# Two feed-forward steps moved ahead of the last attention products, and tiles placed on 64-byte multiples

## The chip, the cores and the metric

The kernel runs on one core of a Trainium2 chip. The metric is the time of one execution on the device in microseconds (us), as the median of several runs. The engines are named as in the profile: PE is TensorE (matmuls; PEld are its weight loads), DVE is VectorE, ACT is ScalarE, POOL is GpSimd, and SP is SyncE, whose queue issues every transfer here.

## The reference

Attention with pooled queries feeds a two-layer feed-forward part. Cut to what matters:

```python
# q, k, v: (8, 8, 1152, 64) float32
q_pool = q.reshape(B, H, S // 2, 2, D).mean(axis=3)          # 576 queries
scores = (q_pool @ k.transpose(0, 1, 3, 2)) / np.sqrt(D)
scores = scores - np.max(scores, axis=-1, keepdims=True)
attn = np.exp(scores)
attn = attn / (np.sum(attn, axis=-1, keepdims=True) + 1e-09)
x = (attn @ v).transpose(0, 2, 1, 3).reshape(4608, 512)      # tokens x d_model
h = x @ w_in                                                 # w_in: 512 x 2048
g = h - np.tanh(h)
out = g @ w_out                                              # w_out: 2048 x 512, out: 4608 x 512
```

## The kernel before

**Attention (lines 155 to 484).** Two heads of one batch make a pair, so there are 32 pairs, worked one after the other. A pair has 18 places: two halves of 288 queries times nine tiles of 128 keys. In the first 18 places each place makes a score tile (`scores`: four matmuls a head, in tiles `kq_h`, `kq_l`, `m_row`, `sel`), ACT takes the exponential into a tile p, and POOL adds the p tiles by threes into six tiles `sum` (`add_p`, twelve additions in all). In the second 18 places come the products with v: for each half, nine key tiles times two heads go into one PSUM tile o, which ACT copies out (`pv_out`, tile `o_s`) and SP stores to `x_dram`. After them the sums of p over the keys are made with 24 matmuls (`sums`), which need POOL's six tiles; ACT copies them out (`s_s`) and SP stores them.

All these PSUM tiles come from one ring of four tiles of 128 x 2 x 512 float32 (`psum`, line 183); a fifth tile takes the place of the first and waits until the last reader of the first is done. Between the places, other work runs from a table (`add`, `run`): the maxima of the next pairs' scores, loads, and the splitting of the weights into a high and a low part by DVE and ACT (class `W`, tiles `w_raw`, `w_off`, `w_t`, `w_hl`). In the pairs 28 to 31 the table also brings in what the feed-forward part needs first: x of chunk 0 (class `X`), which is read back from `x_dram`, divided by the sums and split into `x_h` and `x_l` (done in pair 30), and the weights of the first five steps, which are loaded into tiles whose work is over (`first_weights`): step 0 into `w_raw`, step 1 into `w_off`, step 2 into `w_hl`, steps 3 and 4 into `w_t`, `raw` and `q2`.

**Feed-forward (lines 487 to 611).** The 4608 tokens are worked in nine chunks of 512, each with 16 steps, one for every 128 columns of `w_in`: 144 steps in all. A step has a first product, 12 matmuls of 512 columns into `ps_h` (`hidden`: x_h and x_l are the moving operands, the weights the stationary ones); then h - tanh(h) (`shrink`), on ACT the square `g_u`, two more squares `g_s` and the tanh `g_t`, on POOL a mask `g_m`, on DVE six instructions, of which the fifth (a subtraction, `g_t` from `ps_h`) is the last that reads h and the sixth (a predicated copy) needs the mask; then the result is split into `g_hi` (ACT) and `g_lo` (POOL), one step later; and two steps later the second product, 12 matmuls into four tiles `ps_o` (`second`: g_hi and g_lo are stationary, the weights `wo` move). `ps_h` and a scratch `ps_w` have two tiles each, `ps_o` four. PSUM is given to them only when the ring is closed. At the start of this part SP loads the other 22 weight tiles (`wt`, tile `w`). x of chunk c + 1 is fetched in step 4 of chunk c and prepared on POOL and ACT in steps 7 to 14. x of even chunks lies in pool `xp0`, opened ahead of attention, and x of odd chunks in `xp1`, opened behind it. The last step works in two halves of 256 tokens.

**Order.** Every engine's instructions are held in the order in which the program issues them (`InOrder`, line 27). All instructions are issued through that wrapper, so the profile puts them all on line 37; they are told apart by their tiles.

**Places in SBUF.** Pools are laid out in the order in which they are opened, each tile padded to a multiple of 32 bytes per partition. The order at the bottom is `pc` (two float32), `xp0`, two tiles `x_r`, two tiles `rec` (36 float32 each), `w_raw`, `w_off` (4100 two-byte words), `w_t`, `w_hl`, `raw`, `q2`, and then attention's own pools, whose place the feed-forward part's pools take over later.

Of the kernel before, what the change touches and what calls it, by code (L numbers as in the profile page):

```python
# [7 lines left out]
F32 = mybir.dt.float32  # L8
F32R = mybir.dt.float32r
I32 = mybir.dt.int32  # L10
U16 = mybir.dt.uint16
AF = mybir.ActivationFunctionType
# [34 lines left out]
def attention_ffn_kernel(  # L47
# [30 lines left out]

    const = ctx.enter_context(tc.tile_pool(name="const", bufs=1))
    dram = ctx.enter_context(tc.tile_pool(name="scratch", bufs=1, space=DRAM))  # L80
    pc = const.tile([P, 2], F32, name="pc")
    nc.vector.memset(pc[:, 0:1], A1)
    nc.vector.memset(pc[:, 1:2], A2)

# [25 lines left out]
    class X:  # L110


        def __init__(self, ci):
            self.t0, self.n = chunks[ci]
            self.h = xp[ci % 2].tile([P, NP, 512], F32R, name="x_h")
            self.l = xp[ci % 2].tile([P, NP, 512], F32R, name="x_l")
            self.r = {}
# [24 lines left out]
    rc = {}  # L142

    def fetch_sums(b):
        rc[b] = rcp.tile([P, NP * 2 * SQ // P], F32, name="rec")
        sp.dma_start(rc[b], s_dram[b].rearrange("a h (x n) -> (a h x) n", n=NP * 2 * SQ // P))

    def reciprocals(b):

        dve.tensor_scalar(rc[b], rc[b], 1e-9, None, op0=ALU.add)  # L150
        dve.reciprocal(rc[b], rc[b])
        sp.dma_start(r_dram[b].rearrange("a h (x n) -> (a h x) n", n=NP * 2 * SQ // P), rc[b])


    with ExitStack() as actx:
# [27 lines left out]
        def psum():  # L183
            return ring.tile([P, 2, 512], F32, name="ps")
# [134 lines left out]
        class W:  # L319
# [3 lines left out]
            def load(self):  # L323
                self.raw = wp.tile([P, WN, 2], I32, name="w_raw")

                self.off = wp.tile([P, 4 * WN + 4], U16, name="w_off")
                for dst in (self.raw.rearrange("p n w -> p (n w)").bitcast(U16), self.off[:, 1:4 * WN + 1]):
                    if self.kind == 0:
                        rs, cs = slice(self.i * P, (self.i + 1) * P), slice(4 * self.c, 4 * (self.c + WN))
                        sp.dma_start(dst, w_in[rs, cs])  # L330
                    else:
                        rs = slice(self.i * P, (self.i + 2) * P)
                        sp.dma_start(dst.rearrange("p (a n) -> p a n", a=2), w_out[rs].rearrange("(a p) n -> p a n", a=2))
                self.hw = self.raw[:, :, 1]
                self.mid = self.off[:, 0:4 * WN].bitcast(I32).rearrange("p (n w) -> p n w", w=2)[:, :, 1]
# [123 lines left out]
        def run(pi, place):  # L459
            while at.get((pi, place)):  # L460
                at[pi, place].pop(0)()

        for pi in range(n_pair):
            w = pairs[pi]
            ps = [Half(), Half()]
            for place in range(NS):
                half, kt = divmod(place, KT)
                ps[half].append(scores(w, half, kt))
                add_p(ps[half], half, kt)
                run(pi, place)  # L470
            for place in range(NS):
                half, kt = divmod(place, KT)
                if kt == 0:
                    o = psum()
                for h in range(2):
                    tiled(o[:, 0, 0:HQ], w.v[:, kt, h], ps[half][kt][:, h], h, start=(kt == 0), stop=(kt == KT - 1))
                if kt == KT - 1:
                    pv_out(w, half, o)
                run(pi, NS + place)
                if pi >= 2 and place in (3, 6, 11, 15) and work:  # L480
                    work.pop(0)()
            sums(w, ps)
            run(pi, 2 * NS)
# [1 line left out]


    wt = ctx.enter_context(tc.tile_pool(name="wt", bufs=1))
    gp = ctx.enter_context(tc.tile_pool(name="gp", bufs=2))
    ps_h = ctx.enter_context(tc.tile_pool(name="ps_h", bufs=2, space=PSUM))
    ps_w = ctx.enter_context(tc.tile_pool(name="ps_w", bufs=2, space=PSUM))  # L490
    ps_o = ctx.enter_context(tc.tile_pool(name="ps_o", bufs=4, space=PSUM))
    LAG = 2

    for f in range(NF):
        for which, have in enumerate((wi, wo)):
            if f not in have:
                load_w(wt.tile([P, 1024], F32R, name=f"w{which}_{f}"), f, which)
    xp.append(ctx.enter_context(tc.tile_pool(name="xp1", bufs=1)))

    class Step:  # L500
        pass

    def hidden(s):

        s.h = ps_h.tile([P, 512], F32, name="ps_h")
        mm = [(w, x, c) for w, x in ((0, s.x.h), (0, s.x.l), (1, s.x.h)) for c in range(NP)]
        for k in s.parts:
            for j, (w, x, c) in enumerate(mm):
                pe.matmul(s.h[:, k], wi[s.f][:, w, c], x[:, c, k], start=(j == 0), stop=(j == len(mm) - 1))

    def g_high(s, k=slice(0, 512)):
        act.activation(s.g_h[:, k], s.s1[:, k], AF.Copy)

    def g_low(s, k=slice(0, 512)):
        pool.tensor_tensor(s.g_l[:, k], s.s1[:, k], s.g_h[:, k].bitcast(F32), op=ALU.subtract)

    def shrink(s, before):
        t = lambda name, dt=F32: gp.tile([P, 512], dt, name=name)
        all_ = t("g_u"), t("g_t"), t("g_s1"), t("g_s2"), t("g_m", mybir.dt.uint8), ps_w.tile([P, 512], F32, name="ps_w")
        s.s1 = all_[2]  # L520
        s.g_h = gp.tile([P, 512], F32R, name="g_hi", bufs=LAG + 1)
        s.g_l = gp.tile([P, 512], F32R, name="g_lo", bufs=LAG + 1)
        for k in s.parts:
            shrink_part(s, before, s.h[:, k], *(a[:, k] for a in all_))
            before = None

    def shrink_part(s, before, h, u, th, s1, s2, m, w):
        act.activation(u, h, AF.Square)
        act.activation(s1, u, AF.Square, bias=pc[:, 0:1])
        act.activation(s2, u, AF.Square, bias=pc[:, 1:2])  # L530
        act.activation(th, h, AF.Tanh)
        if before:
            g_high(before)
        pool.tensor_scalar(m, u, T_POLY * T_POLY, None, op0=ALU.is_ge)
        if before:
            g_low(before)
        dve.scalar_tensor_tensor(w, u, -P0, h, op0=ALU.add, op1=ALU.mult)
        dve.scalar_tensor_tensor(w, u, PL, w, op0=ALU.mult, op1=ALU.mult)
        dve.scalar_tensor_tensor(w, s1, P1, w, op0=ALU.add, op1=ALU.mult)
        dve.scalar_tensor_tensor(s1, s2, P2, w, op0=ALU.add, op1=ALU.mult)  # L540
        dve.tensor_tensor(th, h, th, op=ALU.subtract)
        dve.copy_predicated(s1, m, th)

    def second(s, js):
        po = s.chunk.po
        for j in js:
            if len(po) <= j:
                po.append(ps_o.tile([P, DM], F32, name="ps_o"))
            ts = slice(j * P, (j + 1) * P)
            for i, (g, w) in enumerate(((s.g_h, 0), (s.g_h, 1), (s.g_l, 0))):  # L550
                pe.matmul(po[j], g[:, ts], wo[s.f][:, w], start=(s.f == 0 and i == 0), stop=(s.f == NF - 1 and i == 2))

    def store(c, j):
        o = gp.tile([P, DM], F32, name="o_f", bufs=4)
        act.activation(o, c.po[j], AF.Copy)
        sp.dma_start(out[c.t0 + j * P:c.t0 + (j + 1) * P], o)

    class Chunk:
        pass

    def halves():
        return [slice(0, 256), slice(256, 512)]

    steps = []
    xs = x0[0]
    nxt = None
    for ci in range(len(chunks)):
        c = Chunk()
        c.t0, c.po = chunks[ci][0], []
        for f in range(NF):  # L570
            s = Step()
            s.x, s.f, s.chunk, s.parts = xs, f, c, [slice(0, 512)]
            steps.append(s)
        if ci == len(chunks) - 1:
            s.parts = halves()
        xs = None
        for f in range(NF):
            n = ci * NF + f
            s = steps[n]
            hidden(s)  # L580
            if ci + 1 < len(chunks):
                if f == 4:
                    nxt = X(ci + 1)
                    nxt.fetch()
                if f in (4, 5, 9, 11):
                    nxt.fetch_r((4, 5, 9, 11).index(f))
            if n >= 2:
                second(steps[n - 2], range(4))
            shrink(s, steps[n - 1] if n else None)
            if f == 1 and ci:  # L590
                for j in range(4):
                    store(steps[n - 2].chunk, j)
            if n == 4:
                fetch_sums(B - 1)
            if n == 6:
                reciprocals(B - 1)
            if ci + 1 < len(chunks) and 7 <= f < 7 + 2 * NP:
                if f % 2:
                    nxt.times(pool, (f - 7) // 2)
                    nxt.high((f - 7) // 2)  # L600
                else:
                    nxt.low(pool, (f - 7) // 2)
        xs = nxt
# [46 lines left out]
```

## Time and profile before

| | |
|---|---|
| median of 3 runs | 1632.63 us (1632.5 to 1632.68) |
| the profiled execution | 1633.7 us; span 1631.9 us from the first to the last instruction |
| mean granted TensorE clock | 0.996 |
| PE busy | 1586.2 us, 97% of the span |
| DVE, POOL, ACT busy | 1280.5, 1113.3 and 938.5 us |
| attention ends, feed-forward begins | at about 824.9 us |
| transfers | 166.15 MB, mean 102 GB/s |

A row of a timeline gives the start and the length in us, the engine, the line, the operation, the tiles as out<-in, and in brackets the idle time of the engine ahead of it with what ended it. A row of a chain gives start, length and the piece of work. Buffer numbers are left out of names, so `w` stands for each of the 22 tiles loaded late, and `g_s` for `g_s1` and `g_s2`. Matmuls overlap in the profile: the time of a group is read from its start to the start of the next.

### The profile page before, as it was taken

Reading aid. Unit: us, or ns where it says so; the run is one execution under the profiler, and the core shown is the slowest. Engines: PE = TensorE matmul, PEld = TensorE weight load, DVE = VectorE, ACT = ScalarE, POOL = GpSimd, SP = SyncE. Lnnn points to the kernel's source line nnn. Section 1 sums busy time; section 2 is a strip of 40 time slices with the busy share of each in tenths; the row PEclk is TensorE's granted clock in tenths of the full one; section 3 lists DMA queues with packets and bytes.
Section 4 is the critical chain, followed back from the end, with each engine's and each line's share of the span. In section 5 each row is a group of like instructions: output and inputs, shape, how many; then the busy total and the mean of one; then the engine's idle time right before and its main releaser. Section 6 shows DMA issues by size and latency. Waiting matters only on the chain.

```text
span 1631.9 us, 30673 instructions
## 1 busy us (share of the span) xinstructions
PE 1586.2 (97%) x12012; PEld 1228.4 (75%) x12012; DVE 1280.5 (78%) x1621; ACT 938.5 (58%) x1584; POOL 1113.3 (68%) x749
## 2 busy tenths in 40 slices
PE   5999999999999999999999999999999999999998
PEld 4777676776776776777768888888888888888886
DVE  6788888898889898969447777777777777777776
ACT  3565565565655656656535656555555656555554
POOL 3777786776767767778756666666757675666654
PEclk9999999999999999999999999999999999999999
DMA  4335444344453554333471101001010101020000
GB/s 169 107 119 197 167 150 182 133 183 162 155 214 135 200 182 160 131 123 100 152 310 34 65 7 48 31 7 65 13 65 14 65 14 65 13 65 10 30 1 26
DMA packets 79602, 166.15 MB, mean 102 GB/s; under 512 B 11874, under 2 KB 38498, under 8 KB 77410
## 3 DMA queue, kind: packets, MB, share of 16 engines
q1 hardware_dynamic: 79458, 164.20, 28.3%
q8 instruction: 94, 1.54, 0.4%
q14 instruction: 50, 0.41, 0.1%
HBM read 126.12 MB, written 38.04 MB: 101 GB/s over the span
## 4 chain that ended last, share of the span: by engine, by line
PE 83%; DVE 11%; DMA 2%; issue 2%; ACT 2%; POOL 0%; SPq 0%; POOLq 0%; DVEq 0%; ACTq 0%
PE ps L37 35%; PE ps_h L37 24%; PE ps_o L37 24%; DVE mx L37 3%; DVE w_t L37 3%; DVE kq_l L37 1%; DVE w_hl L37 1%; DMA wi_dram<-w_hl 1%; DVE raw L37 1%; ACT w_t L37 1%; DMA m_dram<-tr 0%; SPq L37 0%; DMA q<-in_q_dram 0%; ACT q_last L37 0%; POOL sum L37 0%
## 5 line engine op out<-in xcount | busy, mean ns | idle before, releaser
L37 DVE TENSOR_REDUCE mx<-ps 128x2 f32<-128x768 f32 x448 | 396.6, 924 | 86.9 <-PE ps L37 85.0
L37 POOL TENSOR_TENSOR sum<-p,p 128x576 f32<-128x576 f32 x192 | 300.6, 1566 | 196.7 <-ACT p L37 196.5
L37 ACT ACTIVATE p<-ps 128x576 f32<-128x576 f32 x576 | 353.2, 653 | 112.1 <-PE ps L37 93.7
L37 POOL TENSOR_SCALAR g_m<-g_u 128x512 uint8<-128x512 f32 (+1 forms) x145 | 250.6, 1728 | 197.6 <-ACT g_u L37 182.5
L37 POOL TENSOR_TENSOR sum<-sum,p 128x576 f32<-128x576 f32 x192 | 301.1, 1568 | 29.2 <-ACT p L37 15.1
L37 PE MATMUL ps<-kq_h 64*128 64x288 f32 (+1 forms) x1920 | 289.3, 345 | 28.0 <-DVE mx L37 17.6
L37 PE MATMUL ps<-p,v 128*64 128x288 f32 x2304 | 286.4, 407 | 0.1
L37 DVE SCALAR_TENSOR_TENSOR ps_w<-g_u,ps_h 128x512 f32<-128x512 f32 (+1 forms) x145 | 100.4, 693 | 191.3 <-ACT g_t L37 191.2
L37 PEld LDWEIGHTS ps<-p,v 128*64 128x64 f32 x2304 | 162.6, 137 | 114.4 <-ACT p L37 6.9
L37 POOL TENSOR_TENSOR g_lo<-g_s,g_hi 128x512 fp32r<-128x512 f32 (+1 forms) x145 | 186.6, 1287 | 89.5 <-ACT g_hi L37 89.5
L37 PE MATMUL ps_o<-w,g_hi 128*128 128x512 f32 x792 | 244.5, 390 | 1.0 <-ACT g_hi L37 1.0
L37 PEld LDWEIGHTS ps<-kq_h 64*128 64x128 f32 x1920 | 181.3, 187 | 80.8 <-DVE mx L37 33.0
L37 ACT ACTIVATE g_u<-ps_h 128x512 f32<-128x512 f32 (+1 forms) x145 | 85.8, 591 | 244.0 <-PE ps_h L37 242.3
L37 PE MATMUL ps_h<-x_h,w 128*128 128x512 f32 (+1 forms) x800 | 214.8, 390 | 0.0
L37 ACT ACTIVATE g_s<-g_u,pc 128x512 f32<-128x512 f32 x290 | 193.2, 714 | 11.3
L37 PEld LDWEIGHTS ps_h<-x_h,w 128*128 128x128 f32 x800 | 149.6, 188 | 32.4
L37 PEld LDWEIGHTS ps_o<-w,g_hi 128*128 128x128 f32 x792 | 148.5, 188 | 33.6 <-ACT g_hi L37 1.4
L37 PE MATMUL ps<-kq_l,kq_h 64*128 64x288 f32 x1152 | 171.8, 295 | 0.0
L37 PE MATMUL ps<-kq_h,kq_l 64*128 64x288 f32 x1152 | 171.5, 294 | 0.0
L37 PE MATMUL ps<-m_row,sel 64*128 64x288 f32 x1152 | 171.2, 293 | 0.0
L37 PE MATMUL ps_o<-w,g_lo 128*128 128x512 f32 x396 | 154.8, 391 | 0.6 <-POOL g_lo L37 0.5
L37 DVE COPY_PREDICATED g_s<-g_m,g_t 128x512 f32<-128x512 uint8 (+1 forms) x145 | 108.4, 748 | 15.0
(92 smaller groups left out, 2368.3 us busy)
## 6 DMA issues: line engine op xcount, KB each, us to landing
raw<-in_k_dram SPq DMA_DIRECT2D x32, 576.0 KB
q<-in_q_dram SPq DMA_DIRECT2D x32, 576.0 KB
v<-in_v_dram SPq DMA_DIRECT2D x32, 576.0 KB
x_dram<-o_s SPq DMA_DIRECT2D x32, 288.0 KB
x_l<-x_dram SPq DMA_DIRECT2D x9, 1024.0 KB
out_dram<-o_f SPq DMA_DIRECT2D x36, 256.0 KB
w_raw<-in_w_in_dram SPq DMA_DIRECT2D x8, 1024.0 KB
w_off<-in_w_in_dram SPq DMA_DIRECT2D x8, 1024.0 KB
```

What stands on the lines that cost most here:

```text
L37: i = f(*args, **kwargs)
```

## The change

Two things are changed. First, three tiles get larger sizes, so that every tile starts at a multiple of 64 bytes: `pc` from 8 to 64 bytes, `rec` from 144 to 192 (of which the same part is used), `w_off` from 8200 to 8256.

Second, in the last pair the first product and `shrink` of steps 0 and 1 are issued between the scores and the products with v. Their h and their scratch come from the ring, one ring tile with two halves for the two h, and one for the two scratch tiles, so the last stage takes five ring tiles in place of three. The functions of the feed-forward part and the pool `gp` of its SBUF tiles move ahead of attention, and the feed-forward loop leaves out the two steps' first product and `shrink`. Their second products stay where they were, in steps 2 and 3.

```diff
-    pc = const.tile([P, 2], F32, name="pc")
+    pc = const.tile([P, 16], F32, name="pc")
...
-        rc[b] = rcp.tile([P, NP * 2 * SQ // P], F32, name="rec")
+        rc[b] = rcp.tile([P, 48], F32, name="rec")[:, 0:NP * 2 * SQ // P]
...
+    gp = ctx.enter_context(tc.tile_pool(name="gp", bufs=2))
...
+    class Step:
+        def __init__(self, x, f, chunk):
+            self.x, self.f, self.chunk, self.parts = x, f, chunk, [slice(0, 512)]
...
-                self.off = wp.tile([P, 4 * WN + 4], U16, name="w_off")
+                self.off = wp.tile([P, 4 * WN + 32], U16, name="w_off")
...
+        steps = []
         for pi in range(n_pair):
...
                 run(pi, place)
+            if pi == n_pair - 1:
+                c = Chunk(0)
+                steps = [Step(x0[0], f, c) for f in range(NF)]
+                h, u = psum(), psum()
+                for n in range(2):
+                    steps[n].h, steps[n].w = h[:, n], u[:, n]
+                    hidden(steps[n])
+                    shrink(steps[n], steps[n - 1] if n else None)
             for place in range(NS):
...
     wt = ctx.enter_context(tc.tile_pool(name="wt", bufs=1))
-    gp = ctx.enter_context(tc.tile_pool(name="gp", bufs=2))
...
     for ci in range(len(chunks)):
-        c = Chunk()
-        c.t0, c.po = chunks[ci][0], []
-        for f in range(NF):
-            s = Step()
-            s.x, s.f, s.chunk, s.parts = xs, f, c, [slice(0, 512)]
-            steps.append(s)
+        if ci:
+            c = Chunk(ci)
+            steps += [Step(xs, f, c) for f in range(NF)]
...
-            hidden(s)
+            if n >= 2:
+                s.h, s.w = ps_h.tile([P, 512], F32, name="ps_h"), ps_w.tile([P, 512], F32, name="ps_w")
+                hidden(s)
...
             if n >= 2:
                 second(steps[n - 2], range(4))
-            shrink(s, steps[n - 1] if n else None)
+                shrink(s, steps[n - 1])
```

More of the change, by code (lines that the diff above doesn't have):

```diff
@@ L152, in reciprocals, with hidden @@
         sp.dma_start(r_dram[b].rearrange("a h (x n) -> (a h x) n", n=NP * 2 * SQ // P), rc[b])
+    gp = ctx.enter_context(tc.tile_pool(name="gp", bufs=2))
+    LAG = 2
+    class Step:
+        def __init__(self, x, f, chunk):
+            self.x, self.f, self.chunk, self.parts = x, f, chunk, [slice(0, 512)]
+    def hidden(s):
+        mm = [(w, x, c) for w, x in ((0, s.x.h), (0, s.x.l), (1, s.x.h)) for c in range(NP)]
+        for k in s.parts:
+            for j, (w, x, c) in enumerate(mm):
+                pe.matmul(s.h[:, k], wi[s.f][:, w, c], x[:, c, k], start=(j == 0), stop=(j == len(mm) - 1))
@@ new lines, in g_high, with g_low, shrink @@
+    def g_high(s, k=slice(0, 512)):
+        act.activation(s.g_h[:, k], s.s1[:, k], AF.Copy)
+    def g_low(s, k=slice(0, 512)):
+        pool.tensor_tensor(s.g_l[:, k], s.s1[:, k], s.g_h[:, k].bitcast(F32), op=ALU.subtract)
+    def shrink(s, before):
+        t = lambda name, dt=F32: gp.tile([P, 512], dt, name=name)
+        all_ = t("g_u"), t("g_t"), t("g_s1"), t("g_s2"), t("g_m", mybir.dt.uint8), s.w
+        s.s1 = all_[2]
+        s.g_h = gp.tile([P, 512], F32R, name="g_hi", bufs=LAG + 1)
+        s.g_l = gp.tile([P, 512], F32R, name="g_lo", bufs=LAG + 1)
+        for k in s.parts:
+            shrink_part(s, before, s.h[:, k], *(a[:, k] for a in all_))
+            before = None
@@ new lines, in shrink_part @@
+    def shrink_part(s, before, h, u, th, s1, s2, m, w):
+        act.activation(u, h, AF.Square)
+        act.activation(s1, u, AF.Square, bias=pc[:, 0:1])
+        act.activation(s2, u, AF.Square, bias=pc[:, 1:2])
+        act.activation(th, h, AF.Tanh)
+        if before:
+            g_high(before)
+        pool.tensor_scalar(m, u, T_POLY * T_POLY, None, op0=ALU.is_ge)
+        if before:
+            g_low(before)
+        dve.scalar_tensor_tensor(w, u, -P0, h, op0=ALU.add, op1=ALU.mult)
+        dve.scalar_tensor_tensor(w, u, PL, w, op0=ALU.mult, op1=ALU.mult)
+        dve.scalar_tensor_tensor(w, s1, P1, w, op0=ALU.add, op1=ALU.mult)
+        dve.scalar_tensor_tensor(s1, s2, P2, w, op0=ALU.add, op1=ALU.mult)
+        dve.tensor_tensor(th, h, th, op=ALU.subtract)
+        dve.copy_predicated(s1, m, th)
@@ new lines, in second, with store @@
+    def second(s, js):
+        po = s.chunk.po
+        for j in js:
+            if len(po) <= j:
+                po.append(ps_o.tile([P, DM], F32, name="ps_o"))
+            ts = slice(j * P, (j + 1) * P)
+            for i, (g, w) in enumerate(((s.g_h, 0), (s.g_h, 1), (s.g_l, 0))):
+                pe.matmul(po[j], g[:, ts], wo[s.f][:, w], start=(s.f == 0 and i == 0), stop=(s.f == NF - 1 and i == 2))
+    def store(c, j):
+        o = gp.tile([P, DM], F32, name="o_f", bufs=4)
+        act.activation(o, c.po[j], AF.Copy)
+        sp.dma_start(out[c.t0 + j * P:c.t0 + (j + 1) * P], o)
@@ L155, in attention_ffn_kernel, with __init__, halves @@
+    class Chunk:
+        def __init__(self, ci):
+            self.t0, self.po = chunks[ci][0], []
+    def halves():
+        return [slice(0, 256), slice(256, 512)]
     with ExitStack() as actx:
@@ L491, in attention_ffn_kernel @@
     ps_o = ctx.enter_context(tc.tile_pool(name="ps_o", bufs=4, space=PSUM))
-    LAG = 2
     for f in range(NF):
@@ L498, in attention_ffn_kernel @@
     xp.append(ctx.enter_context(tc.tile_pool(name="xp1", bufs=1)))
[L500 to L566, printed above, removed]
-    for ci in range(len(chunks)):
-        c = Chunk()
-        c.t0, c.po = chunks[ci][0], []
-        for f in range(NF):
-            s = Step()
-            s.x, s.f, s.chunk, s.parts = xs, f, c, [slice(0, 512)]
-            steps.append(s)
+    xs = nxt = None
+    for ci in range(len(chunks)):
+        if ci:
+            c = Chunk(ci)
+            steps += [Step(xs, f, c) for f in range(NF)]
@@ L574, in attention_ffn_kernel @@
         if ci == len(chunks) - 1:
-            s.parts = halves()
+            steps[-1].parts = halves()
         xs = None
```

## Prediction

> **What bounds the kernel now.** I read the page first, for the engine that sets the end.
>
> ```profile
> span 1631.9 us, 30673 instructions
> ...
> PE 1586.2 (97%) x12012; PEld 1228.4 (75%) x12012; DVE 1280.5 (78%) x1621; ACT 938.5 (58%) x1584; POOL 1113.3 (68%) x749
> ...
> PE 83%; DVE 11%; DMA 2%; issue 2%; ACT 2%; POOL 0%; SPq 0%; POOLq 0%; DVEq 0%; ACTq 0%
> ```
>
> TensorE is busy 97% of the span and is 83% of the chain that ended last. So two things can save time: shorter matmuls, and less idle TensorE. The second view is that chain in order of time, around the border of chunk 0 and chunk 1 of the feed-forward part (start, length, what). A piece of 12 matmuls named ps_h is one step's first product, ps_o the second product of the step two before.
>
> ```profile
> 909.35 2.81 PE ps_h L37 x12
> ...
> 914.89 2.79 PE ps_h L37 x12
> ...
> 925.93 2.72 PE ps_h L37 x12
> 928.65 2.80 PE ps_o L37 x12
> ...
> 942.46 2.72 PE ps_h L37 x12
> ```
>
> The reader is to see that equal work takes two lengths. The piece at 909.35 is the last step of chunk 0 and takes 2.81, and 942.46 in chunk 1 takes 2.72. In between, the first step of chunk 1 (weights in w_raw) takes 2.79, the third (weights in w_hl) 2.72; then the second product of step 0 of the chunk, whose moving operand is w_raw, takes 2.80. The groups of TensorE's instructions between 848.2 and 1608 us, shapes apart, say the same (last: busy us, mean ns):
>
> ```profile
> L37 PE MATMUL ps_o<-w_hl,g_hi 128*128 128x512 f32 x72 | 22.2, 390 | 0.0
> ...
> L37 PE MATMUL ps_o<-w_raw,g_hi 128*128 128x512 f32 x64 | 20.1, 396 | 0.0
> L37 PE MATMUL ps_o<-w_off,g_hi 128*128 128x512 f32 x64 | 20.1, 396 | 0.0
> ```
>
> Three sets of tiles are slow: x of the even chunks, w_raw and w_off. By the code's sizes (each padded to 32 bytes, as in the program's list of tiles) pc takes 32 bytes and starts at 16512, so x of the even chunks starts at 16544, w_raw at 37344, w_off at 45536: all 32 past a multiple of 64. w_off is 8224 bytes long, which ends that: w_t, w_hl and everything behind, x of the odd chunks too, lie on multiples of 64. A moving operand is 512 x 4 = 2048 bytes per partition: 32 blocks of 64 bytes, or 33 when it starts half a block off. 33/32 is 1.031, and 2.81/2.72 is 1.033. Blocks of 128 or 256 bytes would give 17/16 = 1.06 or 9/8 = 1.13. So I read the excess as one more 64-byte block per matmul.
>
> The other loss is the handover from attention to the feed-forward part, again from the chain, with the granted clock of one stretch (third number from the end) under it:
>
> ```profile
> 824.94 3.08 PE ps_h L37 x12
> ...
> 833.58 0.61 DVE g_t L37
> 834.19 0.04 issue
> 834.24 5.49 PE ps_h L37 x12
> 839.72 3.06 PE ps_o L37 x12
> 842.79 2.81 PE ps_h L37 x12
> ```
> ```profile
> 833.00:840.50 7.50, 6.26 (x15) 0.54 1.03 419
> ```
>
> Step 2's first product starts at 834.24, when VectorE has last read step 0's result, and then takes 5.49 instead of 2.81, because the clock stood at half (0.54). The chain loses a wait of 3.4 us and 3 us of slow matmuls.
>
> **The change, part 1: multiples of 64.** pc becomes 64 bytes, rec 192, w_off 8256; x, w_raw and w_off then start on multiples of 64. From step 3 of chunk 0 the chain is TensorE's alone up to the last step:
>
> ```profile
> 1608.71 2.81 PE ps_h L37 x12
> ```
> ```profile
> 1614.25 2.87 PE ps_h L37 x24
> ```
>
> From 842.79 (step 3) to 1608.71 (step 142) are 765.92 us for 139 steps. At 2.72 + 2.72 = 5.44, which the odd chunks already show beside the same work on the other engines, they take 756.16: **9.76 us less**. The last step's two halves (2.87) can give 0.15 more, of which I take 0.1, since ScalarE and VectorE set the time from there on. Attention's matmuls lie on multiples of 64 already: nothing. The weights' preparation reads w_raw and w_off on ScalarE and VectorE, each by single 4-byte words 8 bytes apart; no row has such a read at another place. I take 0; for the bounds see the range.
>
> **Part 2: two steps ahead of the last products with v.** Rows of the handover, by engine:
>
> ```profile
> 813.86 8.95 PE L37 MATMUL ps<-p,v 128*64 128x288 f32 x72
> 822.75 1.66 PE L37 MATMUL ps<-sum,ones 128*32 128x288 f32 x24
> 824.94 1.20 PE L37 MATMUL ps_h<-x_h,w_raw 128*128 128x512 f32 x4 [0.53 <-ACT s_s L37]
> ...
> 827.84 0.40 PE L37 MATMUL ps_h<-x_h,w_off 128*128 128x512 f32 x1
> ...
> 842.63 1.09 PE L37 MATMUL ps_h<-x_h,w_t 128*128 128x512 f32 x4
> ```
> ```profile
> 822.13 1.41 POOL L37 TENSOR_TENSOR sum<-sum,p 128x576 f32<-128x576 f32 x1
> ...
> 828.85 1.49 POOL L37 TENSOR_SCALAR g_m<-g_u 128x512 uint8<-128x512 f32 x1 [5.31 <-ACT g_u L37]
> ```
> ```profile
> 834.28 0.74 DVE L37 COPY_PREDICATED g_s<-g_m,g_t 128x512 f32<-128x512 uint8 x1
> ...
> 837.71 0.68 DVE L37 TENSOR_TENSOR g_t<-ps_h,g_t 128x512 f32<-128x512 f32 x1
> ```
>
> Now: from 813.86 to step 3's first matmul at 842.63, 28.77 us. After, on TensorE in order: two first products 2 x 2.72 = 5.44; the products with v 822.75 - 813.86 = 8.89; a new wait W; the sums up to the next start, 824.94 - 822.75 = 2.19 (the wait for s_s stays); step 2's first product 2.72 + 0.09 (the start behind a gap: 827.84 - 824.94 = 2.90 against 2.81); second product 2.72. Together 22.05 + W.
>
> W is the price. The ring has four tiles; the stage now takes five (h, u, two o, sums), so the sums get h's place and need step 1's last read of h, VectorE's subtraction. That stands behind step 0's copy_predicated, which needs g_m, which GpSimd computes only behind its twelve sums: 822.13 + 1.41 = 823.54, plus g_m 1.49 = 825.03. From the copy to the end of the next subtraction are 837.71 + 0.68 - 834.28 = 4.11, with two hand-overs of 0.04 ("issue" above) 829.2. TensorE gets there at 813.86 + 5.44 + 8.89 = 828.19. **W = 1.0**; between 0 (GpSimd ready earlier) and 1.5, as g_m also takes 1.95:
>
> ```profile
> 868.62 1.95 POOL L37 TENSOR_SCALAR g_m<-g_u 128x512 uint8<-128x512 f32 x1 [1.90 <-ACT g_u L37]
> ```
>
> The handover takes 23.05: **5.7 us less**. On ScalarE, g_hi of step 0 waits for the same copy (about 825.9) with both copies out of o and s_s behind it; the first of these is needed by nobody before the feed-forward part's tiles, the others are not ready earlier anyway. VectorE is idle all through the products with v now. On SyncE the order stays, but s_s, and the 22 weight loads behind it, move with the sums, 829.2 - 822.75 = 6.5 us back:
>
> ```profile
> 825.53 0.39 SPq L37 DMA_DIRECT2D w<-wi_dram  x1
> ...
> 845.70 0.32 SPq L37 DMA_DIRECT2D w<-wo_dram  x1
> 846.94 0.37 SPq L37 DMA_DIRECT2D x_l<-x_dram  x1
> ```
> ```profile
> 872.23 1.29 POOL L37 TENSOR_TENSOR x_r<-x_l,x_r 128x512 f32<-128x512 f32 x1
> ```
>
> The 22 loads come 0.96 us apart (20.17/21) where a step of 5.44 uses two, and the first is used only by step 5, so they stay ahead. x of chunk 1 is then fetched at 853.4, and GpSimd takes it up about 6 us earlier than 872.23, near 866. That leaves 12 us for 1024 KB, 2.5 us at the 419 GB/s of the clock's row above. Covered. Moving gp outside the attention stage costs no instruction.
>
> **Sum.** 9.76 + 0.1 + 5.7 = 15.6 us. The profiled execution took 1633.7 (span 1631.9); less 15.6 is 1618.1. The median of the runs, 1632.63, lies 1.07 below that execution: **1617.0**.
>
> **The rivals.**
> D: the clock halves in the new handover, at W and the wait for s_s. Idle stretches of TensorE of 1.5 us did this in attention (a wait of the stretch from 400 to 410 us, and the clock of that stretch and of one more):
>
> ```profile
> PE ps L37 <- DVE mx L37: 1.5, 1, 1.5
> ```
> ```profile
> 400.00:410.00 10.00, 8.43 (x91) 0.83 0.57 209
> 478.00:488.00 10.00, 8.44 (x86) 0.83 0.74 278
> ```
>
> 0.17 of 10 us is 1.7 us lost each time. One or two such: 1618.7 to 1620.4. [...]
>
> A: step 1's first product waits for step 0's readers of h, as both lie in one tile. For it: the last step's first half on ScalarE began only when both halves were written.
>
> ```profile
> 1617.14 0.39 ACT L37 ACTIVATE g_u<-ps_h 128x256 f32<-128x256 f32 x1 [2.56 <-PE ps_h L37]
> ```
>
> Against it: those halves share 2048 bytes, h's two are 2048 apart. Price: TensorE idles from its product's end to the end of VectorE's subtraction, 834.19 - (824.94 + 3.08) = 6.2, and again runs slow for 5.49 - 2.81 + 3.06 - 2.80 = 2.9, while W vanishes: 31.1 instead of 28.77, so 9.9 - 2.3 = 7.6 gained: 1625.0.
>
> B: the place is not what makes these tiles slow, so part 1 does nothing. For it: the slow tiles are also the lowest in memory, which the trace can't part from their offset. Against: the ratio of 33/32. Then only the handover gains, 28.77 - (2 x 2.81 + 8.89 + 2.19 + 2.90 + 2.80 + 0.9) = 5.5: 1627.1. [...]
>
> C, on the other side: what counts is a multiple of 256. All fast tiles of the feed-forward part lie on such now (w_t at 53760 = 210 x 256). The change moves everything from w_t on by 32 + 64 + 32 = 128 bytes (gp alters nothing: 2 x (4 x 2048 + 512) + 6 x 2048 + 4 x 2048 = 37888 = 148 x 256): every step is slow, 2.81 + 2.81 = 5.62 instead of the mean 765.92/139 = 5.51, 15.3 us more, against 5.3 from the handover: 1642.6. It turns the sign from a mean step of 5.55 on. Against it: that ratio again, which would have to be 9/8.
>
> **How the numbers follow.** Forecast 0.73, D 0.09, A 0.07, B 0.08, C 0.03. The forecast's own range: W (-1.0 to +0.5), and attention's two half-clock stretches, which may go or double (3.4 either way): 1613 to 1621. With D that is 0.82; as bounds leak I reach to A: 1613.0 to 1625.5. Faster by over 0.2% (3.3 us, about what a measurement tells from no change) are all but C: 0.95, with 0.02 for an unseen mishap that eats the gain, and 0.03 slower.
>
> **What would show it.** Part 1: ps_h and ps_o pieces of 2.72 in every chunk; wrong if chunk 0 keeps 2.81. Part 2: no wait of TensorE for g_t of over 1.5 us behind the sums' start, a clock of 1.00 through the handover, the sums waiting some 1.0 for VectorE, weight loads from about 832. A idle gap ahead of step 1 means A; steps of 5.62 mean C. The prediction is wrong as a whole if the even chunks' steps don't shorten.

## The result and the profile after

The changed kernel took 1643.56 us (median of 7 runs, 1639.63 to 1648.45), the kernel before 1632.68 beside it on the same chip: ratio 1.0059, 95% interval [1.0041, 1.0077]. It is slower where 15.6 us of gain were forecast. The profiled execution took 1643.69. The page of the changed kernel, the lines that were read first of the kernel before:

```profile
span 1641.8 us, 30667 instructions
...
PE 1588.4 (97%) x12012; PEld 1231.9 (75%) x12012; DVE 1282.7 (78%) x1621; ACT 939.4 (57%) x1584; POOL 1107.3 (67%) x749
...
PE 80%; DVE 11%; DMA 4%; issue 2%; ACT 2%; SPq 0%; POOL 0%; POOLq 0%; DVEq 0%; ACTq 0%
```

TensorE is as busy as it was, and a transfer has come onto the chain (DMA 4% instead of 2%): something is waited for that was not. The chain at the border of chunk 0 (even) and chunk 1 (odd) says what became of the lengths of the products:

```profile
915.60 2.76 PE ps_h L37 x12
918.36 2.77 PE ps_o L37 x12
...
937.60 2.72 PE ps_h L37 x12
940.32 2.80 PE ps_o L37 x12
```

The even chunk's step is 2.76 + 2.77 = 5.53 us, where it was 5.54. The second product with w_raw (940.32) still takes 2.80. All these tiles now start at multiples of 64.

The handover is in the timeline of TensorE, with the granted clock of one stretch (third number from the end) under it:

```profile
821.50 1.19 PE L37 MATMUL ps<-x_h,w_raw 128*128 128x512 f32 x4
...
830.59 2.07 PE L37 MATMUL ps<-x_h,w_off 128*128 128x512 f32 x4 [6.04 <-DVE g_t L37]
...
835.42 8.95 PE L37 MATMUL ps<-p,v 128*64 128x288 f32 x72
...
846.49 1.21 PE L37 MATMUL ps_h<-x_h,w_hl 128*128 128x512 f32 x4 [0.53 <-ACT s_s L37]
...
852.15 1.08 PE L37 MATMUL ps_h<-x_h,w_t 128*128 128x512 f32 x4
```
```profile
830.00:835.00 5.00, 4.41 (x11) 3.49 (x12) 1.28 (x2) 0.00 (x0) 2.68 (x2) 0.54 0.00 0
```

Step 1's first product waits 6.04 us for VectorE's subtraction of step 0, and then runs at a clock of 0.54. The transfers come in once more in step 6, on the chain:

```profile
866.31 10.20 DMA w<-wo_dram
876.51 0.02 issue
876.53 7.05 DMA rec<-s_dram
883.58 0.02 issue
883.60 0.19 DVE rec L37
...
887.70 3.02 PE ps_h L37 x12
```
```profile
887.70 1.19 PE L37 MATMUL ps_h<-x_h,w 128*128 128x512 f32 x4 [2.21 <-DVE g_t L37]
```
```profile
1618.90 2.76 PE ps_h L37 x12
```

The first instruction of the reciprocals on VectorE waits 5.0 us for rec, and TensorE idles 2.21 us behind it. The last row is step 142 on the chain, which puts a start 0.16 later than the timeline does (842.79 against 842.63 for step 3 before). With these rows the 9.9 us of span split:

| stretch | before | after | difference | forecast |
|---|---|---|---|---|
| start to the last score | 813.86 | 821.50 | +7.64 | 0 |
| last score to step 3 | 28.77 | 30.65 | +1.88 | -5.7 |
| step 3 to step 142 | 765.92 | 766.59 | +0.67 | -9.76 |
| step 142 to the end | 23.2 | 22.9 | -0.3 | -0.1 |

The largest part lies where no cost was expected, in attention. Pair by pair (from the start of one pair's products with v to the next's, the pairs counted from 1) it comes in steps. Pairs 3, 9, 12 and 21 lose 1.24 to 1.34 us each, and each has a stretch of half clock that the other profile lacks; pair 18 gains 1.36, where the kernel before had one. Windows around the first, of the kernel before and of the changed one:

```profile
104.00:108.00 4.00, 3.98 (x56) 3.74 (x56) 3.64 (x4) 2.72 (x5) 2.54 (x3) 1.00 0.97 393
```
```profile
104.00:108.00 4.00, 4.00 (x39) 4.00 (x39) 2.41 (x4) 2.15 (x4) 2.17 (x2) 0.57 0.99 413
```

Attention has 6 such stretches after and had 2 before. Pairs 4, 16 and 19 lose 0.63, 0.61 and 0.83 with no change of the clock, pair 13 gains 0.49 with none, and pair 7 loses 2.63, of which one half-clock stretch is about half. There VectorE waits for the store of w_hl; the same store in the kernel before and in the changed one:

```profile
195.62 4.02 DMA wi_dram<-w_hl
```
```profile
196.97 5.20 DMA wi_dram<-w_hl
```

### The profile page after: what moved, and what is told of

It is laid out like the page before. It is cut to its first block, busy times and chain, and to the rows that moved or that the text cites. A ratio compares the mean times of both kernels' runs of the same rounds, so it can differ in the third digit from the quotient of the medians.

```text
span 1641.8 us, 30667 instructions
## 1 busy us (share of the span) xinstructions
PE 1588.4 (97%) x12012; PEld 1231.9 (75%) x12012; DVE 1282.7 (78%) x1621; ACT 939.4 (57%) x1584; POOL 1107.3 (67%) x749
## 4 chain that ended last, share of the span: by engine, by line
PE 80%; DVE 11%; DMA 4%; issue 2%; ACT 2%; SPq 0%; POOL 0%; POOLq 0%; DVEq 0%; ACTq 0%
PE ps L37 35%; PE ps_h L37 23%; PE ps_o L37 23%; DVE mx L37 3%; DVE w_t L37 3%; DMA w<-wo_dram 2%; DVE kq_l L37 1%; DVE w_hl L37 1%; DMA wi_dram<-w_hl 1%; DVE raw L37 1%; ACT w_t L37 1%; DMA rec<-s_dram 0%; SPq L37 0%; DMA m_dram<-tr 0%; DMA q<-in_q_dram 0%
## 5 line engine op out<-in xcount | busy, mean ns | idle before, releaser
L37 POOL TENSOR_TENSOR sum<-sum,p 128x576 f32<-128x576 f32 x192 | 297.3, 1548 | 33.4 <-ACT p L37 19.4
```

What stands on the lines that cost most here:

```text
L37: i = f(*args, **kwargs)
```

## The experiments

Two questions were open: which property of a place makes a matmul fast, and what each of the other stalls is. "Remainder" below is a tile's start in bytes modulo 256.

**128 instead of 64.** The kernel before with larger pads: x of the even chunks and nearly all other tiles get remainder 0, w_raw and w_off get 128.

```diff
-    pc = const.tile([P, 2], F32, name="pc")
+    pc = const.tile([P, 32], F32, name="pc")
-        rc[b] = rcp.tile([P, NP * 2 * SQ // P], F32, name="rec")
+        rc[b] = rcp.tile([P, 48], F32, name="rec")[:, 0:NP * 2 * SQ // P]
-                self.off = wp.tile([P, 4 * WN + 4], U16, name="w_off")
+                self.off = wp.tile([P, 4 * WN + 64], U16, name="w_off")
```

> The kernel before with pc, rec and w_off enlarged so that x of the even chunks starts at 16640 and w_raw at 37504, both multiples of 128. Theory U (the unit is 128 bytes: at multiples of 64 that are odd, these tiles stay slow): every feed-forward step takes 5.44 us in every chunk and the time falls by about 10 us against before, to 1622.6. Theory P (the place of these tiles low in memory makes them slow, not the offset): the even chunks keep 5.53 to 5.54 us a step and the time stays within 2 us of before.

1626.26 against 1635.29, ratio 0.9944 [0.9922, 0.9967]: a median step of 5.44 in every chunk. But the groups of TensorE between 860 and 1600 us (last: busy us, mean ns) keep two sets slow, w_raw and w_off, of which the first is shown beside w_hl:

```profile
L37 PE MATMUL ps_h<-x_h,w_raw 128*128 128x512 f32 x64 | 17.5, 395 | 0.0
...
L37 PE MATMUL ps_h<-x_h,w_hl 128*128 128x512 f32 x64 | 17.1, 389 | 0.0
```

w_raw lies on a multiple of 128 here and is slow (395 ns); w_hl, whose remainder is that of x, is not (389). That rival B is wrong follows too: moving a tile does change its speed.

**The tile or its offset.** The kernel before, with 32 bytes put ahead of x of the odd chunks, whose steps take 5.44. This x then has remainder 32, where w and g have 0:

```diff
+    dve.memset(xp[1].tile([P, 8], F32, name="pad"), 0.0)
```

> The kernel before with x of the odd chunks moved up by 32 bytes (a small tile ahead of it in its pool, written once). U: the odd chunks' steps grow from 5.44 to about 5.54 us, some 6 us in all. P: they stay at 5.44.

The odd chunks went from 5.44 to 5.56 a step; one run, 1640.99. On the chain, one step of chunk 1:

```profile
944.29 2.80 PE ps_h L37 x12
947.10 2.76 PE ps_o L37 x12
```

The offset decides, not being low in memory.

**Part 1 alone.** The kernel before with the changed kernel's three sizes and nothing else.

```diff
+    pc = const.tile([P, 16], F32, name="pc")
+        rc[b] = rcp.tile([P, 48], F32, name="rec")[:, 0:NP * 2 * SQ // P]
+                self.off = wp.tile([P, 4 * WN + 32], U16, name="w_off")
```

> Part 1 of the change alone: the tile sizes of the changed kernel in the kernel before. The trace of the changed kernel shows 5.53 us a step in even chunks. U and P both: no gain, within 1 us of before. My prediction's step (a unit of 64 bytes): 9.9 us less.

1638.82, ratio 1.0014 [1.0002, 1.0026]: the sizes alone gain nothing. Even chunks 5.533, odd 5.44, as in the changed kernel, and attention is longer by 12.9 us in its profile (last score at 826.77), with 7 stretches of half clock (mean granted clock 0.990). That execution, of 1644.61, was the longest of the ten, so 12.9 us are more than a typical one loses.

**A ring tile for each early step.** The changed kernel, with step 0's h and scratch in one ring tile and step 1's in another: still five tiles in the stage.

```diff
-                h, u = psum(), psum()
                 for n in range(2):
-                    steps[n].h, steps[n].w = h[:, n], u[:, n]
+                    hu = psum()
+                    steps[n].h, steps[n].w = hu[:, 0], hu[:, 1]
```

> The changed kernel with one ring tile for each of the two early steps (h in its first half, the scratch in its second), instead of one tile for both h and one for both scratches. Theory T (step 1's first product waits for the readers of step 0's h because both lie in one tile): the 6.05 us wait of TensorE ahead of step 1 and the half clock behind it are gone, the handover from the scores' end to step 3 falls from 30.65 us to about 22.3, and the time by about 8 us against the changed kernel; what stays is the wait of VectorE for the last sums' transfer in step 6 (5.0 us, 2.2 us of it on TensorE). Rival (the wait comes from VectorE's and ScalarE's order, not from the tile): the wait stays.

1634.27, ratio 0.9989 [0.9974, 1.0004] where the changed kernel has 1.0059. Its timeline and a window over the handover:

```profile
822.82 1.10 PE L37 MATMUL ps<-x_h,w_raw 128*128 128x512 f32 x4
823.75 1.10 PE L37 MATMUL ps<-x_h,w_off 128*128 128x512 f32 x4
...
826.65 8.95 PE L37 MATMUL ps<-p,v 128*64 128x288 f32 x72
...
843.39 1.08 PE L37 MATMUL ps_h<-x_h,w_t 128*128 128x512 f32 x4
```
```profile
820.00:843.50 23.50, 22.97 (x161) 15.61 (x158) 8.54 (x13) 10.96 (x21) 16.05 (x12) 1.00 0.21 72
```

Step 1 starts right behind step 0, the clock stays at 1.00, and from the last score (820.86) to step 3 it is 22.53 us instead of 30.65. So the wait was for the tile, not for h: as the program orders its waits, the readers of one half hold up the writer of the other. The wait for rec in step 6 is still there (4.6 us on VectorE, 1.81 idle on TensorE).

**All remainders 0.** Theory R now: what counts is that the tiles of a matmul have the same remainder, whichever. The kernel before with pc at 128 bytes, one rec tile of 256 and w_off at 8448.

```diff
+    rcp = ctx.enter_context(tc.tile_pool(name="rcp", bufs=1))
+    pc = const.tile([P, 32], F32, name="pc")
+        rc[b] = rcp.tile([P, 64], F32, name="rec")[:, 0:NP * 2 * SQ // P]
+                self.off = wp.tile([P, 4 * WN + 128], U16, name="w_off")
```

> The kernel before with pc 128 bytes, one rec tile of 256, w_off 8448, so that x, w_raw, w_off, w_t, w_hl and all tiles of the feed-forward part lie on multiples of 256. Theory R (a matmul is fast when its moving operand and the tiles it works beside have the same remainder modulo 256): every chunk 5.44 a step, and the steps with w_raw and w_off, which were still at 2.79 with those at 128, go to 2.72; from step 3 to step 142 756 to 757 us instead of 765.9, 1622 to 1625 us in all. Theory U (multiples of 128 are enough): no gain beyond that with 128, 1626. Theory S (a store of w_hl is late when w_hl does not start at a multiple of 256): the last score ends at 813 to 816 us, as before.

1624.33, ratio 0.9945 [0.9931, 0.9958]. From step 3 to step 142 it is 756.16 us, every step 5.44, w_raw now as fast as the rest:

```profile
L37 PE MATMUL ps_h<-x_h,w_raw 128*128 128x512 f32 x64 | 17.1, 389 | 0.0
```

The last score came at 818.93 and not at 813 to 816, in the longest of the six executions (1628.84, mean granted clock 0.993): five stretches of half clock, and 1.55 more in pair 7; but pairs 4, 16 and 19 are as before (-0.03, 0.02, -0.05).

**All remainders 160.** The same with pc left at 8 bytes, so that not one of these tiles is on a multiple of 64.

```diff
-    pc = const.tile([P, 32], F32, name="pc")
+    pc = const.tile([P, 2], F32, name="pc")
```

> The same, but pc left at 8 bytes: every tile of the feed-forward part lies 160 past a multiple of 256, none on a multiple of 64. Theory R: still 5.44 a step in every chunk, 756 to 757 us from step 3 to step 142. Any theory of an absolute multiple (64, 128 or 256): every step slow, 5.54 to 5.62, 769 to 781 us. Theory S: attention is longer, the last score ends at 818 to 826 us instead of 814; without S 813 to 816.

Again 756.16 us from step 3 to step 142, every step 5.44:

```profile
L37 PE MATMUL ps_o<-w_raw,g_hi 128*128 128x512 f32 x64 | 19.7, 389 | 0.0
...
L37 PE MATMUL ps_h<-x_h,w_hl 128*128 128x512 f32 x64 | 17.1, 389 | 0.0
```

This settles it: no multiple is needed, equal remainders are. (The tiles lie 96 bytes lower than in the kernel above, so wherever the first pool starts, the two kernels can't both be on multiples of 64.) The time is 1630.34, 0.9977 [0.9964, 0.9989], as attention is longer (last score 821.88), with pairs 4, 16 and 19 losing 0.90, 0.84 and 0.74. The store of w_hl in pair 4, on the chains of the kernel before and of this one:

```profile
120.51 3.95 DMA wi_dram<-w_hl
```
```profile
120.01 4.86 DMA wi_dram<-w_hl
```

**w_hl alone at remainder 0, the rest at 160.** 96 bytes of filler ahead of w_hl and 160 behind it.

```diff
+                    if not W.pads:
+                        W.pads.append(wp.tile([P, 24], F32, name="pad_a"))
                     self.hl = wp.tile([P, 2, WN], I32, name="w_hl")
+                    if len(W.pads) == 1:
+                        W.pads.append(wp.tile([P, 40], F32, name="pad_b"))
```

> The kernel with all tiles 160 past a multiple of 256, but w_hl alone put at a multiple of 256 (96 bytes ahead of it, 160 behind). Theory S (the store of w_hl is late when w_hl does not start at a multiple of 256): the 0.7 to 0.9 us that pairs 4, 16 and 19 lost each with w_hl at 160, 64 past and the like go back to 0, and VectorE's wait for that store falls from 6 us to 3 to 5. Rival: they stay, as something else in the layout makes them. Theory R: step 2 of each chunk, whose weights lie in w_hl, is slow again (2.75 to 2.81 for its first and second product), all other steps 2.72.

One run, 1627.25. The losses of pairs 4, 16 and 19 are gone (0.01, 0.00, -0.03), and the products that use w_hl, 389 ns a matmul in the kernel above, are now the only ones over 390:

```profile
L37 PE MATMUL ps_h<-x_h,w_hl 128*128 128x512 f32 x64 | 17.6, 396 | 0.0
L37 PE MATMUL ps_h<-x_h,w_raw 128*128 128x512 f32 x64 | 17.1, 389 | 0.0
```

One tile moved shows both effects at once: the store is short from remainder 0, the matmul from equal remainders.

**Part 2 alone.** The changed kernel with the sizes of before.

```diff
-    pc = const.tile([P, 16], F32, name="pc")
+    pc = const.tile([P, 2], F32, name="pc")
-        rc[b] = rcp.tile([P, 48], F32, name="rec")[:, 0:NP * 2 * SQ // P]
+        rc[b] = rcp.tile([P, NP * 2 * SQ // P], F32, name="rec")
-                self.off = wp.tile([P, 4 * WN + 32], U16, name="w_off")
+                self.off = wp.tile([P, 4 * WN + 4], U16, name="w_off")
```

> The changed kernel with the tile sizes of before: part 2 alone. The shared tile of h costs what it did with both parts: TensorE idles 6 us ahead of step 1 and the clock halves, 30.7 us from the last score to step 3 instead of 28.8; the wait for rec costs 2.4. Theory S: attention is as before, the last score at 813 to 817. In all 2 to 5 us slower than before, ratio 1.001 to 1.003. Rival (the moved steps or the earlier pool lengthen attention): the last score at 820 or later, ratio 1.004 to 1.007.

1638.42, ratio 1.0027 [1.0016, 1.0039]. The wait ahead of step 1 is the same:

```profile
824.19 2.08 PE L37 MATMUL ps<-x_h,w_off 128*128 128x512 f32 x4 [6.05 <-DVE g_t L37]
```

30.53 us from the last score (815.09) to step 3; attention as before, pairs 4, 16 and 19 unchanged. So part 2 costs its share by itself, and attention's loss belongs to part 1.

**The three repairs together.** The changed kernel with own ring tiles, all remainders 0, and the reciprocals in step 12.

```diff
-            if n == 6:
+            if n == 12:
                 reciprocals(B - 1)
```

> The changed kernel with an own ring tile for each of the two early steps, the reciprocals of the last batch in step 12 instead of 6, and all tiles on multiples of 256. From the others: last score 813 to 816, 22.5 us to step 3, 756 to 757 to step 142, 23 behind: a time of 1615 to 1619 us, ratio 0.989 to 0.991. If S is wrong, attention stays at 820 and the time is 1623. If the wait for rec comes from the load itself and not from where it is asked for, 2 us more.

1617.85, ratio 0.9904 [0.9892, 0.9917]; 22.34 us to step 3. But step 3 to step 142 took 758.14, 2 us too many. VectorE no longer waits for rec; now the chain shows GpSimd and ScalarE late with x of chunk 1 (they wait 1.8 and 5.1 us for x_r), whose fetch stands behind the same loads:

```profile
852.53 12.03 DMA x_l<-x_dram
...
865.06 2.36 DMA x_r<-r_dram
867.43 0.01 issue
867.43 0.63 ACT x_h L37
```

So the rival in this expectation was right in substance: the time that the reciprocals were asked for was not the cause.

**The later weights behind x.** That kernel, with the weights of steps 9 to 15 loaded in step 5, behind the fetch of x.

```diff
+                if f < 9:
+                    load_w(t, f, which)
+                else:
+                    late.append((t, f, which))
...
+            if n == 5:
+                for a in late:
+                    load_w(*a)
```

> The best kernel so far (own ring tiles, all at multiples of 256, reciprocals in step 12), with the weights of steps 9 to 15 loaded behind the fetch of x of chunk 1 and not ahead of it. Theory Q (the 2.1 us lost in chunk 0 are the queue of loads on SyncE, whose end whoever is behind it waits for): chunk 0 runs at 5.44 a step throughout, 756 to 757 us from step 3 to step 142 instead of 758.1, 2 us less in all: 1615 to 1617. Rival: the loss stays, or the late weights are missed by step 9: 1618 or more.

The second of the two has one line changed back:

```diff
-            if n == 12:
+            if n == 6:
                 reciprocals(B - 1)
```

> The same with the reciprocals back in step 6, where the changed kernel has them. Theory Q: no loss either, within 0.5 us of the kernel with them in step 12, as rec is now fetched ahead of 14 loads. Rival (the reciprocals in step 6 are late in themselves): a wait of VectorE for rec of 2 us or more, and TensorE idle for 1 to 2 us in chunk 0.

1617.63, ratio 0.9904 [0.9888, 0.9921], and with the reciprocals back in step 6 1617.65, 0.9907 [0.9893, 0.9922]. In both, VectorE no longer waits for rec nor ScalarE for x_r, and from step 3 to step 142 it is 756.16 us. Of the first, SyncE's queue, then two rows of TensorE (its timeline and its chain):

```profile
836.25 0.69 SPq L37 DMA_DIRECT2D x_l<-x_dram  x1
...
843.01 0.33 SPq L37 DMA_DIRECT2D rec<-s_dram  x1
...
850.40 0.58 SPq L37 DMA_DIRECT2D w<-wi_dram  x1
```
```profile
837.39 0.84 PE L37 MATMUL ps_h<-x_h,w_t 128*128 128x512 f32 x3
```
```profile
1593.71 2.72 PE ps_h L37 x12
```

So the queue of loads was the cause, wherever the reciprocals stand. In the medians the 2 us don't show against the kernel with the reciprocals moved: attention took 2.7 us longer in the first one's profile (last score 815.04 against 812.34), with 4 stretches of half clock against 1 (mean granted clock 0.996 against 0.998).

## Why the prediction was wrong

- **Part 1, the unit.** "So I read the excess as one more 64-byte block per matmul" failed. The rows were read rightly (x of the even chunks, w_raw and w_off slow), and so was the price, 756.16 us for the 139 steps; the cause was not. 33/32 against 1.033 was a coincidence. Before the change those three tiles had remainders 160, 224 and 224 and all else that TensorE reads there 0; the change gave them 192, 64 and 64 and the rest 128, so they still differed from it. The 9.76 us did not come (5.540 to 5.533 for an even step). Rival C took its unit as an absolute one: the odd chunks, now all at 128, stayed at 5.44 and refute that. That its price, 1642.6, lies next to the measured 1643.56 is chance.
- **Part 2, rival A.** "h's two are 2048 apart" was the wrong argument. A happened: 30.65 where it was priced at 31.1, with no W behind it. The price of the work itself was right: with own tiles the handover took 22.34 to 22.53, where the sum without W is 22.05. W = 1.0 was not tested: in the changed kernel the wait of A comes first, and with own tiles the sums take step 0's tile and need not wait for step 1's readers.
- **Part 2, "Covered".** Only x was followed behind the 22 loads. rec, fetched in step 4 behind the same loads and used by VectorE in step 6, was not looked for; it cost 2.21 us of TensorE. Two steps fewer stood between the start of the loads and their users, and this term was left out. x itself would have been late next, as the run with the reciprocals in step 12 showed (ScalarE waited 5.1 us for x_r).
- **Attention, "nothing".** The whole of attention was set to 0 as its matmuls do not change. Its store of w_hl does: 57856 is a multiple of 256, 57984 is not. In four kernels with w_hl at remainder 128 or 160, pairs 4, 16 and 19 lost 0.61 to 0.90 each; in eight others at 0 nothing beyond 0.05, but for one 0.52. That is 2.1 us of the 7.64. In all, VectorE waited 6.2 to 8.7 us for w_hl's stores to `wi_dram` in the four, and 3.1 to 5.5 in the others. Why the store takes longer from there (4.86 against 3.95 us in pair 4) was not shown; that the place of w_hl decides was shown by moving w_hl alone.
- **In part open.** The rest of the 7.64 is mostly four more stretches of half clock. How many there are varies between executions of one kernel: the kernel before took 1631.61 to 1639.59 in 20 runs beside the first experiments, at a mean granted clock of 0.997 to 0.992, where one stretch takes off 0.001 (half of 3.4 us in 1632). Behind the first 30 us, the profiles of both kernels have eight idle stretches of TensorE in attention, of 1.5 to 2.0 us and 75 to 78 us apart; two of the eight are followed by half clock in the kernel before and five in the changed one, whose sixth follows a new idle stretch (1.48 us), in pair 7. Which of the eight are followed goes with how the clock's grid falls on them (last section), so part of the loss in this one profile is the luck of the execution. Probably not all of it: in the medians part 1 alone ran at 0.993 (ten runs) where the kernel before beside it ran at 0.995, and all remainders 160 at 0.994 against 0.9965, which by the 0.001 is an estimate of two to three more stretches, 2.6 to 3.9 us. With all remainders 0 it is 0.996 against 0.9965. How the later stores bring them was not shown, nor how much of the measured 10.9 us they are.
- **What held.** Rival D's mechanism, that 1.5 us of idle TensorE can halve the clock, and TensorE as the bound: with the stalls and the unequal remainders gone, the time is 1617.6. That the forecast of 1617.0 lies beside it is partly luck, as other means got there: equal remainders, own tiles and later loads.

## What to carry to other kernels

When like matmuls take two lengths (2.72 and 2.81 us for 12 here), list the start of every operand's tile and compare the tiles with one another before looking for a multiple; then move one tile and look again. A PSUM tile was one thing to wait for here, whatever its halves held (6.04 us ahead of step 1), so give each producer its own. When work is moved ahead, follow every transfer that is issued behind the same queue to its user, not only the largest one.

## What the runs showed of the hardware

- A matmul of 512 float32 columns takes 389 ns in its group's mean and 12 take 2.72 us when the moving and the stationary tile start at the same place modulo 256 (0 and 0, 128 and 128, 160 and 160), and 2.75 to 2.81 when they differ by 32, 64, 96 or 128. Tiles at odd and at even multiples of 256 mix freely (389 ns in every group with all remainders 0), so 256 is the period. In some kernels the neighbouring product is slowed although its own tiles agree (2.77 in the even chunks after). It is its first matmuls that are slowed: from start to start the first ten of the 12 take 224 to 236 ns there instead of 227, and in the kernel before only the first three (mostly 230 to 233). Why, is not known.
- In attention half-clock stretches last 3.4 us each and cost 1.3 (at the handover two follow each other, 6.8 us). In the profile after they start at 104.2, 206.6, 257.8 and 336.3 us, 30, 15 and 23 times 3.413 apart, so they lie on a fixed grid; the two of the kernel before, at 406.7 and 481.8 us, are 22 times 3.413 apart. The idle stretches in attention are mostly 1.5 to 2.0 us long, less than one interval of the grid. How much of one stretch falls into one interval told the cases apart: with each profile's own grid laid over attention from 30 us on, in the profiles of both kernels, half clock followed 7 of the 9 intervals in which TensorE was idle for 1.5 us or more (1.51 to 2.01), and 1 of the 450 with less (1.499 us). None of the seven idle stretches of 1.5 us or more that a border of the grid parts into less was followed by it, so one kernel can have other numbers of half-clock stretches in other executions: the mean granted clock of the kernel before went from 0.992 to 0.997 in the 20 runs.
